# AFNO kernel: inverse DFT on 64 x 64 quarters of the array in plain 32-bit form, and the remainder block spread into its rows by on-chip transfers

## The chip, the cores and the metric

One Trainium2 chip, one core of it. The metric is the device time of one execution of the whole program in microseconds (us). A run with the profiler on leaves a trace, from which all lines marked as profile are taken; times in it count from the first instruction. PE is TensorE with its matmuls, PEld its weight loads, DVE is VectorE, ACT is ScalarE, POOL is GpSimd, SP is SyncE, which here does nothing but issue DMAs in order.

## What is computed

A block of a spectral network over 4096 rows of 640 columns, followed by a SwiGLU feed-forward part. The part that matters here is the spectral one:

```python
def _A_ref(x, w1, b1, w2, b2):
    Xf = jnp.fft.rfft2(x, axes=(1, 2))            # (1, 1, 4096, 640): a real DFT over the 4096 rows
    z = Xf.reshape(B, H, Wf, NB, BS)              # NB = 4 blocks of BS = 160 columns
    hr = relu(zr @ w1[0] - zi @ w1[1] + b1[0])    # one complex layer for each block
    hi = relu(zi @ w1[0] + zr @ w1[1] + b1[1])
    or_ = hr @ w2[0] - hi @ w2[1] + b2[0]         # a second one
    oi_ = hi @ w2[0] + hr @ w2[1] + b2[1]
    # soft shrink of both by 0.01
    return irfft2(or_ + 1j * oi_, s=(H, W), axes=(1, 2))

x = x + ga * _A_ref(layernorm(x) * (1 + ca) + sa)
x = x + gb * ((silu(h @ w_gate) * (h @ w_up)) @ w_down)      # h = layernorm(x) * (1 + cb) + sb
```

The six vectors `sa, ca, ga, sb, cb, gb` come from `silu(c) @ w_mod`. Results are wanted in 32-bit precision.

## The kernel before

**Two steps of the DFT.** 4096 = 128 x 32. A first DFT over 128 points (`dft_a`, L432) is done as matmuls on the normalised rows, whose results go to memory (`s1`, by `write_s1`, L354) and come back as tiles `g`, sorted by frequency. From there the work runs in 8 chunks (`ch`) of 512 frequencies; `tb` holds the constants of a second DFT over 32 points.

**A chunk.** `stage_b` (L594) does the second DFT for the five column tiles of 128: tiles 0 to 3 hold the first 128 columns of the blocks, tile 4 the remainders, the last 32 columns of all four blocks (32 partitions for each). `evac_b` (L603) brings a tile 0 to 3 out of PSUM as `z`, in two parts: a high part rounded to the short form `fp32r` by ACT (L607) and the difference by DVE (L608). The product of two such sums is made of three `fp32r` matmuls instead of one plain 32-bit matmul. `evac_rh` and `evac_rl` (L622, L633) do the same for tile 4, but block by block, for real and imaginary part apart: each instruction takes 32 partitions of PSUM and writes them to the partitions where the first layer wants them. So a tile `rz` for a block holds on 128 partitions: 32 high real, 32 high imaginary, 32 low real, 32 low imaginary. A chunk takes eight instructions on ACT (L630) and eight on DVE (L640) for it.

**The layers.** `stage_l1` (L646) makes three products `pl` for a block: two with eight matmuls (six with `z` and the weights `w1a` and `w1b`, two with `rz` and `w1c`; L661) and one with five (L674), and takes them through the relu to `h` and `r`. `stage_l2` (L695) makes the second layer from them, with frequencies on the partitions, into `tt`, whose two halves are real and imaginary part.

**Back.** `move_x` (L727) copies from `tt` to `xx` by two DMAs on SP, so that real and imaginary part of 64 frequencies stand on 128 partitions. `shrink_parts` and `shrink` (L735, L740) do the soft shrink, `shrink_high` and `shrink_low` (L748, L755) split `xx` into `xh` (ACT, L752) and `xl` (DVE, L757). `stage_i` (L759) does the inverse DFT over 32 points: for each half of the 640 columns three `fp32r` matmuls of 128 x 128 (L768 to L770) with the constants `bm`, an evacuation to `co` (L771), and one DMA from POOL to `s2` (L772). The constants hold zeros outside of two blocks of 64 x 64, as frequencies of odd and of even number do not mix. The last chunk takes another way: `inverse_last` (L815) uses plain 32-bit matmuls on 64 rows of `tt` (L825) with the constants `bx`.

**What sets the order.** All of this stands in a hand-written order (`manual_schedule`), and each engine runs its instructions in that order. The loop at L837 goes over passes `p` = 4 `ch` + `b`: the first layer of pass `p`, second DFT and evacuation for later passes, the second layer of `p - 1`, the shrink of `p - 6` and the inverse DFT of `p - 7`. Ahead of the loop stand the first chunk's `stage_b`, `evac_b` and `evac_r` (L792 to L798). Ahead of these, from L491 to L531, SP gets a long row of DMAs: writes of `s1`, loads of `g` and `tb` of chunk 1, and the constants `idn`, `tx` and `bx`. PSUM tiles come from named banks: `p1`, `p2`, `p3` with two buffers each, and `b0` and `b1`.

After the spectral part (from about 306 us on) the feed-forward part runs. It is the same in both kernels.

Of the kernel before, what the change touches and what calls it, by code (L numbers as in the profile page):

```python
# [6 lines left out]
F32 = mybir.dt.float32  # L7
# [6 lines left out]
P = 128  # L14
# [32 lines left out]
def constants():  # L47
# [8 lines left out]
    fa = np.zeros((N1, 128))  # L56
# [56 lines left out]
    bm = bm.reshape(2, 128, 128)  # L113
    bi = bm[1].reshape(2, 64, 128)

    bx = np.tile(bm[1].reshape(2, 64, 128).transpose(1, 0, 2), (2, 1, 1)).reshape(128, 256)
    bmh, bml = _hl(bm)
    bm = np.stack([bmh, bml], axis=1)
    bm = np.ascontiguousarray(bm.transpose(2, 0, 1, 3)).reshape(128, 2 * 2 * 128)
# [38 lines left out]
def layouts(given):  # L158
    out = {}
    for n in ("A_w1", "A_w2"):  # L160
        w = given[n].transpose(2, 0, 1, 3)
        rows = [w[128:160, ::1 - 2 * (q % 2)] for q in range(4)]
        out[n] = np.ascontiguousarray(np.stack([w[0:128], np.concatenate(rows)]))
# [10 lines left out]
def body(tc, x, w1, b1, w2, b2, wg, wu, wd, c, wm, k_fa, k_tb, k_tx, k_bm, k_bx, k_ga, k_ge, k_id, out, dbg=None):  # L174
# [27 lines left out]
    with ExitStack() as top:  # L202
# [35 lines left out]
        with ExitStack() as af:  # L238
# [4 lines left out]
            bm = wp.tile([P, 2, 2, 128], F32R, name="bm")  # L243
            tx = wp.tile([P, 2], F32, name="tx")
            lp = af.enter_context(tc.tile_pool(name="lp", bufs=1))
            fa = lp.tile([P, 128], F32, name="fa")
# [9 lines left out]
            def prep_weights(raw, wa, wb, wc, split):  # L256
# [11 lines left out]
                for o in range(2):  # L268
                    for oh, ol, n, src in parts(o):
# [6 lines left out]
                                 (wc, h, l, rr[:, o, :, e], 1.0 if o else sgn[:, 0:1])]  # L276
# [63 lines left out]
            with tc.tile_pool(name="sp", bufs=1) as sp:  # L340
# [91 lines left out]
                def dft_a(t):  # L432

                    xnr = xas[t].rearrange("p a (b e) -> p a b e", b=NB)
                    for n, i in enumerate((0, 1, 2, 3, 4) if t < 7 else (4, 0, 1, 2, 3)):
# [3 lines left out]
                        mm(pa, fa, xnr[:, i, :, 0:128] if i < 4 else xnr[:, :, :, 128:160], start=True, stop=True)  # L439
# [15 lines left out]
                for t in range(8):  # L455
# [5 lines left out]
                    if t == 6:  # L461

                        prep1 = prep_weights(raws[1], w1a, w1b, w1c, True)
# [58 lines left out]
            prep2 = prep_weights(raws[2], w2a, w2b, w2c, False)  # L522
# [80 lines left out]
            def evac_b(ch, t):  # L603
                pb = pbs[ch, t]
                z = lp.tile([P, 2, 2, 258], F32R, tag="z", bufs=4, name=f"z{ch}_{t}")
# [10 lines left out]
            def evac_r(ch, b, part=None):  # L616
                if part != 1:
                    evac_rh(ch, b)
                if part != 0:
                    evac_rl(ch, b)  # L620

            def evac_rh(ch, b):  # L622
                pb = pbs[ch, 4]
                if b == 0:
                    rzs[ch] = hp.tile([P, NB, 258], F32R, tag="rz", bufs=2, name=f"rz{ch}")
                    if ch == CE:
                        pool.tensor_copy(rzs[ch][:, :, 257], zero.rearrange("p a b c d -> p (a b c d)")[:, 0:4])
                q = slice(32 * b, 32 * b + 32)
                for i in range(2):
                    act.activation(rzs[ch][32 * i:32 * i + 32, b, 0:256], pb[q, i, :], AF.Identity,  # L630
                                   scale=ca1[q, 4:5])

            def evac_rl(ch, b):  # L633
                pb = pbs[ch, 4]
                r = rzs[ch]
                q = slice(32 * b, 32 * b + 32)
                for i in range(2):
                    rh = slice(32 * i, 32 * i + 32)
                    rl = slice(64 + 32 * i, 96 + 32 * i)
                    dve.scalar_tensor_tensor(r[rl, b, 0:256], pb[q, i, :], ca1[q, 4:5],  # L640
                                             f32(r[rh, b, 0:256]), op0=OP.mult, op1=OP.subtract)
                    if ch == CE:
                        pool.tensor_copy(r[rh, b, 0:257:256], f32(edge[q, 0, 4, i]))
                        pool.tensor_copy(r[rl, b, 0:257:256], f32(edge[q, 1, 4, i]))
# [1894 lines left out]
```

## Time and profile before

| | us |
|---|---|
| median of three runs | 1415.19 |
| the runs | 1413.05, 1418.73, 1415.19 |
| span of the profiled execution, first to last instruction | 1409.5 |
| normalisation and first DFT | 0 to 55.8 |
| first chunk starts | 55.8 to 80 |
| passes of the loop | 80 to 284 |
| last chunk, hand-over | 284 to 306 |
| feed-forward part | 306 to 1409.5 |

The profiled execution's own time is not listed beside its span; the three runs lie 3.6 to 9.2 us over it. The stretches were chosen from the timeline. In a row of the busy time by stretch stand the length, then for each engine the busy time and the number of its instructions, the granted clock of TensorE (1.00 is full), the share of the DMA engines that is busy, and GB/s. In a row of a timeline stand start, length, engine, line, operation, what is written and read, the shape and the number of instructions merged, and in brackets the idle time ahead and what ended it. In a row of one tile or line stand minimum, median and maximum in ns. A matmul lasts longer than the distance to the next one, since matmuls overlap in the array: distances are read from starts.

### The profile page before, as it was taken

The page shows a single profiled execution, that of the slowest core. Times are in us where ns is not written, and L with a number is a line of the kernel's source. Part 1 is how long each engine was busy: PE and PEld are TensorE (multiplying, and loading weights), DVE is VectorE, ACT ScalarE, POOL GpSimd, SP SyncE. Part 2 cuts the span into 40 slices and gives each one's busy share as a digit, 9 for nine tenths or more (in the row PEclk, how much of TensorE's full clock was granted, in tenths as well). Part 3 has the DMA queues.
Part 4 walks back from the last instruction along what each step waited for, and adds up shares of the span by engine and source line. Part 5 has one row for each costly group of instructions (what it writes and reads, how often), then busy time and mean ns, then how long its engine had stood idle before and what let it go on. Part 6 is the DMA issues. An engine that isn't in the chain of part 4 may idle for free. (4 is left out here: it accounts for less than half of the span.)

```text
span 1409.5 us, 23754 instructions
## 1 busy us (share of the span) xinstructions
PE 1382.5 (98%) x8410; PEld 1310.7 (93%) x8410; DVE 1067.8 (76%) x1861; ACT 765.0 (54%) x1542; POOL 604.6 (43%) x683
## 2 busy tenths in 40 slices
PE   6899999999999999999999999999999999999998
PEld 2599999967999889899999999999999999999998
DVE  8889888889888888649787668678678757375644
ACT  6879999755555554436454345546164624262341
POOL 5700200157766594326445534447153624042241
PEclk9999999999999999999999999999999999999999
DMA  9876466675998897898877998696998668956634
GB/s 371 310 244 211 157 196 193 203 232 170 327 353 308 308 335 263 293 368 308 308 225 281 375 330 288 236 326 230 375 330 309 217 218 282 350 194 217 199 115 149
DMA packets 171016, 377.34 MB, mean 268 GB/s; under 512 B 22193, under 2 KB 81649, under 8 KB 168882
## 3 DMA queue, kind: packets, MB, share of 16 engines
q1 hardware_dynamic: 161794, 359.28, 73.6%
q0 software_dynamic: 6800, 13.93, 3.1%
q10 hardware_dynamic: 2304, 2.62, 0.5%
q8 instruction: 66, 1.08, 0.3%
q14 instruction: 52, 0.43, 0.1%
HBM read 269.48 MB, written 96.80 MB: 260 GB/s over the span
## 5 line engine op out<-in xcount | busy, mean ns | idle before, releaser
L1442 DVE TENSOR_TENSOR wb<-r,wb 128x768 fp32r<-128x768 f32 (+3 forms) x170 | 170.4, 1013 | 13.5 <-ACT wb L1435 13.3
L2050 PE MATMUL pw<-h,wt 128*128 128x384 f32 x412 | 139.3, 338 | 0.6 <-ACT s_y L2069 0.6
L2052 PE MATMUL pw<-h,wt 128*128 128x384 f32 x412 | 138.3, 336 | 0.0
L2051 PE MATMUL pw<-h,wt 128*128 128x384 f32 x412 | 138.1, 335 | 0.0
L1435 ACT ACTIVATE wb<-r 128x768 fp32r<-128x768 f32 (+3 forms) x168 | 104.5, 639 | 56.3 <-PE pw L2063 41.7
L2351 PE MATMUL pc<-wq,L 128*128 128x320 f32 x846 | 132.7, 309 | 0.9 <-DMA wq<-wqd 0.9
L2110 POOL TENSOR_TENSOR sg<-s_x,sg 128x384 f32<-128x384 f32 x24 | 30.0, 1250 | 234.5 <-DVE s_x L2076 234.5
L2351 PEld LDWEIGHTS pc<-wq,L 128*128 128x128 f32 x846 | 126.3, 188 | 1.1 <-DVE x L2308 1.1
L2130 DVE TENSOR_TENSOR L<-sg,L 128x384 fp32r<-128x384 f32 x144 | 101.0, 725 | 27.7 <-ACT L L2126 27.2
L2069 ACT ACTIVATE s_x<-pw 128x384 f32<-128x384 f32 x52 | 25.6, 492 | 164.2 <-PE pw L2052 162.3
L2050 PE MATMUL pw<-h,wb 128*128 128x384 f32 x312 | 105.0, 336 | 0.0
L2051 PE MATMUL pw<-h,wb 128*128 128x384 f32 x312 | 104.4, 335 | 0.0
L2052 PE MATMUL pw<-h,wb 128*128 128x384 f32 x312 | 104.4, 335 | 0.0
L2121 POOL TENSOR_TENSOR sg<-sg,sg 128x384 f32<-128x384 f32 x72 | 91.9, 1276 | 23.4 <-DVE L L2130 20.0
L1973 PE MATMUL pg<-ht,wb 128*128 128x512 f32 x260 | 101.8, 392 | 0.0
L2351 PE MATMUL pe<-wq,L 128*128 128x320 f32 x648 | 101.7, 309 | 0.0
L1974 PE MATMUL pg<-ht,wb 128*128 128x512 f32 x260 | 101.3, 390 | 0.0
L1975 PE MATMUL pg<-ht,wb 128*128 128x512 f32 x260 | 101.2, 389 | 0.0
L2267 PE MATMUL pd<-wq,a 128*128 128x320 f32 x632 | 96.8, 310 | 0.0
L2351 PEld LDWEIGHTS pe<-wq,L 128*128 128x128 f32 x648 | 96.6, 188 | 0.0
L2267 PEld LDWEIGHTS pd<-wq,a 128*128 128x128 f32 x632 | 93.5, 188 | 0.5
L772 POOL DMA_DIRECT2D s<-co x28 | 15.7, 559 | 175.9 <-ACT co L771 175.9
(317 smaller groups left out, 3914.1 us busy)
## 6 DMA issues: line engine op xcount, KB each, us to landing
wq<-wqd SPq DMA_DIRECT2D x83, 640.0 KB, 6.1
wt<-td SPq DMA_DIRECT2D x103, 512.0 KB, 5.4
hs<-ho SPq DMA_DIRECT2D x52, 512.0 KB, 5.2
h<-hs SPq DMA_DIRECT2D x32, 768.0 KB, 7.9
td<-wt SPq DMA_DIRECT2D x25, 512.0 KB, 6.3
r<-in_B_w_gate_dram SPq DMA_DIRECT2D x24, 384.0 KB, 4.4
r<-in_B_w_up_dram SPq DMA_DIRECT2D x24, 384.0 KB, 4.3
xx<-tt SPq DMA_DIRECT2D x56, 160.0 KB, 3.3
```

The costliest lines, as they stand in the source:

```text
L1435: def high(ks, e=slice(0, c), copy=lambda o, i: act.activation(o, i, AF.Copy)):
L1442: dve.tensor_tensor(wbs[t, n][:, 1, ks, e], raw[t, n][:, ks, e], f32(wbs[t, n][:, 0, ks, e]), op=OP.subtract)
L1973: mm(b, wh, hh, start=(kk == 0), stop=False)
L1974: mm(b, wh, hl, start=False, stop=False)
L1975: mm(b, wl, hh, start=False, stop=(kk == 4))
L2050: mm(b, w(0, kp), a[:, kp, 0], start=start and kp == 0, stop=False, skip_group_check=not start)
L2051: mm(b, w(0, kp), a[:, kp, 1], start=False, stop=False, skip_group_check=not start)
L2052: mm(b, w(1, kp), a[:, kp, 0], start=False, stop=kp == 1, skip_group_check=not start)
L2121: pool.tensor_tensor(o, x, y, op=op)
L2130: dve.tensor_tensor(o[:, 1], raws[j], f32(o[:, 0]), op=OP.subtract)
L2267: mm(b[:, :320], l, m, start=start and i == 0, stop=stop and i == len(s) - 1)
L2351: mm(o[:, :320], ls[q][:, x, k], w[:, q, y], start=start and q == 0 and n == 0, stop=q == 1 and n == 2, skip_group_check=not start)
```

## The change

1. **Remainder block.** `evac_b` now serves tile 4 too: one instruction on ACT and one on DVE for a chunk, into `z` under a tag of its own (`zr`, one buffer). `move_r` then spreads it by four DMAs on SP, one for each block: 32 partitions with four rows of 256 each go to 128 partitions of `rz`. The rows of `rz` now stand in another order, and the rows of `w1c` with them; their signs come from a column that is added to `fa`.
2. **Inverse DFT.** `bm` holds only the 64 x 64 blocks in plain 32-bit form. `stage_i` takes `xx` directly, by four plain 32-bit matmuls: rows `u` (64 partitions) and columns `e` (320) each pick a quarter of the array. `shrink_high` and `shrink_low` go, and the inverse DFT comes one pass earlier (`p - 6`). The result goes to `s2` by two DMAs on POOL. `move_x` copies with one DMA in place of two. `bm` is loaded by SP, not by POOL.
3. **Order.** Tile 4 is made first in a chunk, also in the first one. `pb` alternates between banks `b0` and `b1`. In the very first block (`ch` = 0, `b` = 0) the products with `z` are issued for all three `pl` ahead of those with `rz`.

```diff
-    fa = np.zeros((N1, 128))
+    fa = np.zeros((N1, 130))
+    fa[:, 128] = (-1.0) ** np.arange(N1)
...
-    bmh, bml = _hl(bm)
...
+    bm = np.stack([bm[:, :, u, :, u].reshape(2, 64, 64) for u in range(2)])
+    bm = bm.reshape(2, 2, 2, 32, 64).transpose(0, 3, 2, 1, 4).reshape(128, 128)
...
-                      bank0(1 if t == 4 else 0, [P, 2, 256], f"pb{ch}_{t}"))
+                      bank0(len(pbs), [P, 2, 256], f"pb{ch}_{t}"))
...
-            def evac_rh(ch, b):
...
-            def evac_rl(ch, b):
...
+            def move_r(ch):
+                rzs[ch] = hp.tile([P, NB, 258], F32R, tag="rz", bufs=2, name=f"rz{ch}")
+                NN = width(ch)
+                for b in range(NB):
+                    nc.sync.dma_start(f32(rzs[ch][:, b, :NN]), f32(zs[ch, 4][32 * b:32 * b + 32, :, :, :NN]))
...
+                if not ch and not b:
+                    for o, n in ((0, 6), (1, 6), (2, 4)):
+                        products(o, 0, n)
...
-                for r in range(2):
-                    nc.sync.dma_start(xx[64 * r:64 * r + 64, :], tts[ch, q][64 * h:64 * h + 64, r, :])
+                nc.sync.dma_start(xx, tts[ch, q][64 * h:64 * h + 64])
...
-            def shrink_high(ch, i):
...
-            def shrink_low(ch, i):
...
             def stage_i(ch, i):
-                xh, xl, _ = xxs[ch, i]
-                for hf in range(2):
...
-                    mm(pi[:, :320], bm[:, kd, 0, :], xh[:, e], start=True, stop=False)
-                    mm(pi[:, :320], bm[:, kd, 0, :], xl[:, e], start=False, stop=False)
-                    mm(pi[:, :320], bm[:, kd, 1, :], xh[:, e], start=False, stop=True)
...
+                for e in range(2):
+                    for u in range(2):
+                        k = slice(64 * u, 64 * u + 64)
+                        mm(pi[u][64 * e:64 * e + 64, :320], bm[k, kd], xx[k, 320 * e:320 * e + 320], start=True, stop=True)
+                for u in range(2):
+                    act.activation(co[:, u], pi[u][:, :320], AF.Copy)
+                for e in range(2):
+                    pool.dma_start(s2[4 * J:4 * J + 4, :, 320 * e:320 * e + 320].rearrange("(u k) n d -> (k n) u d", u=2),
+                                   co[64 * e:64 * e + 64])
...
-            for b, tag in ((0, None), (4, None), (1, "p2")):
+            for b, tag in ((4, None), (0, None), (1, "p2")):
                 stage_b(0, b, tag)
...
+            evac_b(0, 4)
+            move_r(0)
             for b in range(2):
                 evac_b(0, b)
-                evac_r(0, b)
...
-                on(stage_i, p - 7)
+                on(stage_i, p - 6)
...
-                    pool.dma_start(bm.rearrange("p a b c -> p (a b c)"), k_bm)
+                    nc.sync.dma_start(bm.rearrange("p a b -> p (a b)"), k_bm)
```

**SP, where the first chunk starts.** Before, from the last write of `s1` (shown as `s<-xa`) to the first copies of `xx`:

```order
L355 DMA s<-xa_122 64x4x640
L508 DMA idn<-in_k_id_dram 128x128
L509 DMA tx<-in_k_tx_dram 128x2
L531 DMA bx<-in_k_bx_dram 128x256
L308 DMA g_898<-s 128x1x2560
L298 DMA tb_900<-in_k_tb_dram 128x512
L536 DMA wm_0_987<-in_w_mod_dram 128x640
```

Now, from the same write on:

```order
L354 DMA s<-xa_122 64x4x640
L507 DMA idn<-in_k_id_dram 128x128
L508 DMA tx<-in_k_tx_dram 128x2
L530 DMA bx<-in_k_bx_dram 128x256
L619 DMA rz_666<-z_4_663 128x1x256 x4
L862 DMA bm<-in_k_bm_dram 128x128
L619 DMA rz_857<-z_4_854 128x1x256 x4
L307 DMA g_892<-s 128x1x2560
```

The four transfers of the first chunk's `rz` come in behind the load of `bx` and all writes of `s1`, and those of the second chunk ahead of the load of `g`.

**PE, from the second DFT of the first chunk on.** Before (`pb` second DFT, `pl` first layer of block 0):

```order
L600 MATMUL pb_0_646<-tb_408,g_453 128x2x64 x4
L600 MATMUL pb_4_651<-tb_408,g_453 128x2x64 x4
L600 MATMUL pb_1_656<-tb_408,g_453 128x2x64 x4
L661 MATMUL pl_0_0_685<-z_0_663,w1a 128x256 x3
L661 MATMUL pl_0_0_685<-z_0_663,w1b 128x256 x3
L661 MATMUL pl_0_0_685<-rz_666,w1c 128x256 x2
L661 MATMUL pl_0_1_699<-z_0_663,w1a 128x256 x3
```

Now:

```order
L599 MATMUL pb_4_646<-tb_408,g_453 128x2x64 x4
L599 MATMUL pb_0_651<-tb_408,g_453 128x2x64 x4
L599 MATMUL pb_1_656<-tb_408,g_453 128x2x64 x4
L646 MATMUL pl_0_0_684<-z_0_671,w1a 128x256 x3
L646 MATMUL pl_0_0_684<-z_0_671,w1b 128x256 x3
L646 MATMUL pl_0_1_685<-z_0_671,w1a 128x256 x3
L646 MATMUL pl_0_1_685<-z_0_671,w1b 128x256 x3
L646 MATMUL pl_0_2_686<-z_0_671,w1a 128x256 x2
L646 MATMUL pl_0_2_686<-z_0_671,w1b 128x256 x2
L646 MATMUL pl_0_0_684<-rz_666,w1c 128x256 x2
L646 MATMUL pl_0_1_685<-rz_666,w1c 128x256 x2
L646 MATMUL pl_0_2_686<-rz_666,w1c 128x256
```

The 16 products with `z` now stand ahead of the five with `rz`; nothing else of PE stands between them and the second block.

**PE, one call of the inverse DFT in the loop.** Before, between the second layer (`pc`) and the next first layer:

```order
L711 MATMUL pc_2_1_1309<-w2c,r_1_2_1196 128x320 x2
L768 MATMUL pi_0_1320<-xh_0_1210,bm 128x320
L769 MATMUL pi_0_1320<-xl_0_1211,bm 128x320
L770 MATMUL pi_0_1320<-xh_0_1210,bm 128x320
L768 MATMUL pi_1_1325<-xh_0_1210,bm 128x320
L769 MATMUL pi_1_1325<-xl_0_1211,bm 128x320
L770 MATMUL pi_1_1325<-xh_0_1210,bm 128x320
```

Now, at the same place of a pass:

```order
L698 MATMUL pc_1_1_1200<-w2c,r_1_1_1089 128x320 x2
L744 MATMUL pi_0_1211<-xx_0_1044,bm 64x320
L744 MATMUL pi_1_1212<-xx_0_1044,bm 64x320
L744 MATMUL pi_0_1211<-xx_0_1044,bm 64x320
L744 MATMUL pi_1_1212<-xx_0_1044,bm 64x320
L646 MATMUL pl_3_0_1227<-z_3_1019,w1a 128x256 x3
```

Six matmuls of the full array become four on quarters of it, which write two banks in turn.

More of the change, by code (lines that the diff above doesn't have):

```diff
@@ L461, in body @@
                     if t == 6:
[L463 removed]
+                        prep1 = prep_weights(raws[1], w1a, w1b, w1c, True, fa[:, 128:129])
                         for job in prep1[:6]:
@@ L667, in stage_l1 @@
                     hs.append(h)
-                pl = (bank0(1, [P, 512], f"pl{ch}_{b}_2") if 4 * ch + b > LAST else
-                      ps.tile([P, 512], F32, tag="p3", name=f"pl{ch}_{b}_2"))
-                cs = slice(512, 640)
-                seq = [(w1a, z[:, 0, 0, :NN]), (w1a, z[:, 1, 0, :NN]), (w1b, z[:, 0, 1, :NN]),
-                       (w1b, z[:, 1, 1, :NN]), (w1c, r[:, :NN])]
-                for i, (l, m) in enumerate(seq):
-                    mm(pl[:, :NN], l[:, b, cs], m, start=(i == 0), stop=(i == len(seq) - 1))
+                pl = pls[2]
+                products(2, 0 if ch or b else 4)
                 u0 = hp.tile([64, 258], F32, tag="u0", bufs=2, name=f"u0_{ch}_{b}")
```

127 lines of the change are left out of this document (41 added, 86 removed).

## The prediction

> **What bounds the kernel now.** I read the page first, then the busy time by stretch, PE's waits, and last the timelines of PE and SP. Tiles stand without their numbers.
>
> ```profile
> PE 1382.5 (98%) x8410; PEld 1310.7 (93%) x8410; DVE 1067.8 (76%) x1861; ACT 765.0 (54%) x1542; POOL 604.6 (43%) x683
> 55.80:80.00 24.20, 21.29 (x166) 20.50 (x167) 20.40 (x38) 16.58 (x36) 12.30 (x9) 1.00 0.99 372
> 80.00:260.00 180.00, 179.86 (x1408) 178.81 (x1407) 158.10 (x306) 168.39 (x347) 17.51 (x52) 1.00 0.59 189
> 284.00:306.00 22.00, 21.32 (x91) 14.04 (x91) 19.30 (x39) 8.46 (x17) 9.13 (x16) 1.00 0.65 204
> 306.00:1409.50 1103.50, 1092.98 (x6478) 1055.47 (x6475) 801.36 (x1303) 514.00 (x1040) 529.36 (x531) 1.00 0.80 277
> ```
>
> The columns after the length are PE, PEld, DVE, ACT, POOL, clock, DMA share, GB/s. From 80 to 260 us (inverse DFT and both spectral layers) PE is busy 179.86 of 180 us: there only a change of PE's own work counts. From 306 on nothing is edited, and PE is busy 99%: what the first stage gains or loses arrives at the end whole. DMA is full (0.99) from 55.8 to 80, where the first chunk starts. PE's waits there:
>
> ```profile
> PE pc L711 <- DVE r L691: 1.1, 1, 1.1
> PE pb L600 <- DVE z L608: 0.7, 1, 0.7
> PE pc L711 <- DVE w2c L286: 0.5, 1, 0.5
> PE pl L661 <- DVE rz L640: 0.5, 1, 0.5
> ```
>
> **1. The first remainder transfer.** Today ACT and DVE write the rows of `rz` themselves, and PE waits 0.5 us for them. Here are the first evacuation, PE at the first layer, and SP at that time:
>
> ```profile
> 57.01 0.69 ACT L607 ACTIVATE z<-pb,ca 128x512 fp32r<-128x512 f32 x1 [1.76 <-PE pb L600]
> 57.73 0.75 DVE L608 SCALAR_TENSOR_TENSOR z<-pb,ca,z 128x512 fp32r<-128x512 f32 x1 [1.31 <-ACT z L607]
> 58.51 0.60 PE L661 MATMUL pl<-z,w1a 128*128 128x256 f32 x3
> 59.99 0.48 PE L661 MATMUL pl<-rz,w1c 128*128 128x256 f32 x2 [0.52 <-DVE rz L640]
> 60.30 0.51 PE L661 MATMUL pl<-z,w1a 128*128 128x256 f32 x3
> ...
> 61.84 1.05 PE L600 MATMUL pb<-tb,g 128*128 128x128 f32 x8
> 66.30 11.38 SPq L355 DMA_DIRECT2D s<-xa  x10
> 77.72 1.37 SPq L508 DMA_DIRECT2D idn<-in_k_id_dram  x1
> 79.14 1.18 SPq L509 DMA_DIRECT2D tx<-in_k_tx_dram  x1
> 80.42 0.95 SPq L531 DMA_DIRECT2D bx<-in_k_bx_dram  x1
> 81.61 0.57 SPq L308 DMA_DIRECT2D g<-s  x1
> L731 SPq DMA_DIRECT2D xx<-tt x56: 466/591/1482, 92.3 to 268.7; - x56
> DMA to landing us min/median/max: 2.4/3.3/4.8
> ```
>
> The change gives this write to SP. In SP's order (shown with the change) the four transfers of `rz` stand behind the load of `bx`, whose issue ends at 80.42 + 0.95 = 81.37 us; ahead of it SP issues without a pause, ten writes of `s` in 11.38 us. Nothing of the change moves or shortens those. The source is ready long before: the evacuation of the remainder block takes the place of the first one (ACT from 57.01, DVE done at 58.5). So the first transfer is issued at 81.4. No row shows this transfer; the nearest is `xx<-tt`, also from SBUF to SBUF, with 2.4 to 4.8 us to landing. I take its median 3.3: landing at 84.7 (83.8 to 86.2).
>
> PE needs it much sooner. The new order runs 16 products without `rz` first. Thirteen products took 61.84 - 60.30 = 1.54 us, 0.118 each; the low half of `z` is ready about 59.3 (the second ACT step starts when the second block is there, near 57.9, and takes 0.69, DVE 0.75), so they end near 61.2. Then PE's queue is blocked: every later matmul stands behind the five products with `rz`. These end at 84.7 + 5 x 0.118 = 85.3 instead of 61.84: **+23.5 us** (22.6 to 25.0). Nothing covers it, as all of PE's further work hangs on this layer. Behind the transfers on SP stand `bm`, `g` and `tb`, used passes later.
>
> Two smaller terms go with it. DVE makes the weights `w2` during the stall, and the bank of `pb` now alternates, so 1.1 + 0.7 + 0.5 = 2.3 us of waits can go: **-2.3** (0 to -2.3). And PE restarts cold:
>
> ```profile
> L439 PE MATMUL pa<-xa,fa 128*128 128x512 f32 x6 | 5.5, 1088 | 8.0 <-ACT xa L418 8.0
> L439 PE MATMUL pa<-xa,fa x6: 592/592/807, 13.3 to 15.6; 128*128 128x512 f32 x6
> ```
>
> After the idle 8 us at the kernel's start the first six matmuls took 5.3 us (8.0 to 13.3), 0.88 each; the next came 0.46 apart, though the page's granted clock reads full. That loses 6 x 0.42 = 2.5 us. I take **+2.2** (0 to 2.7), as part of the slow stretch falls where PE would wait for ACT anyway. By the Trainium skill (page "TensorE: Matmul & The Clock Gate", section "Part 1: The HAM clock gate") an idle window of about 3.4 us halves PE's clock and a busy one of that length restores it; by that figure the loss would be an estimated 1.7 us, and the trace agrees on the half, not on the length.
>
> **2. The inverse DFT on PE.** 28 calls (one write of `s<-co` each):
>
> ```profile
> L772 POOL DMA_DIRECT2D s<-co x28 | 15.7, 559 | 175.9 <-ACT co L771 175.9
> 203.66 0.31 PE L768 MATMUL pi<-xh,bm 128*128 128x320 f32 x1
> ...
> 204.54 0.52 PE L661 MATMUL pl<-z,w1a 128*128 128x256 f32 x3
> 297.75 1.24 PE L986 MATMUL py<-cfrr,et 128*128 128x320 f32 x4
> 298.82 1.24 PE L983 MATMUL py<-tt,et 128*128 128x320 f32 x4
> 284.81 1.35 PE L825 MATMUL pi<-tt,bx 64*128 64x320 f32 x8 [0.53 <-ACT co L771]
> 286.10 0.41 PE L768 MATMUL pi<-xh,bm 128*128 128x320 f32 x1
> 286.35 0.31 PE L769 MATMUL pi<-xl,bm 128*128 128x320 f32 x1
> 287.51 2.51 PE L825 MATMUL pi<-tt,bx 64*128 64x320 f32 x8
> ```
>
> Now: six matmuls in 204.54 - 203.66 = 0.88 us. After: four plain 32-bit matmuls, each of which PE runs as two (L986: two in the program for each block, four in the trace), at (298.82 - 297.75) / 4 = 0.268 us. One after the other they would take 8 x 0.268 = 2.14 us. But L825 shows two halves of the array at work at once: eight matmuls on 64 rows, half of them on the upper rows, take 1.35 us at 284.81, near 4 x 0.268 + 0.16 = 1.23 (one lasts 1.24 - 3 x 0.268 = 0.43, 0.16 past its slot), and 2.51 where a wait keeps the halves apart. The columns are not split in any row of before. If all four quarters run together the body is 2 x 0.268 = 0.54 us, if only row halves do, 1.07. I take 0.54, plus 0.08 for starts that stand one behind the other.
>
> The switch costs too. At 286.10 PE goes back to the full array: the slot of the last L825 ends at 284.81 + 1.35 - 0.16 = 286.00, so it starts 0.10 late, and its successor comes 0.25 later instead of 0.147: 0.2 us lost. The way in loses 0.12 in the body (1.35 against 1.23); I take 0.15. A call so costs 0.54 + 0.08 + 0.35 = 0.97 us against 0.88: 28 x 0.09 = **+2.5 us**, between 28 x (0.54 - 0.88) = -9.5 (no switch cost) and, with row halves only, 28 x (1.07 + 0.35 - 0.88) = +15.1.
> The Trainium skill (page "TensorEngine Tiling (Array Packing)", section "Key Properties") says "Changing tiling mode (not just tile) drains the TensorE", which speaks against the change; the 0.2 us at 286.10 agrees; without it the term would fall toward the -9.5. The same section lets the tiles load and multiply independently; the trace shows this of the two row halves alone.
>
> **3. Work taken off ACT and DVE.**
>
> ```profile
> L630 ACT ACTIVATE rz<-pb,ca x64: 448/468/472, 57.9 to 260.0; 32x256 fp32r<-32x256 f32 x64
> L640 DVE SCALAR_TENSOR_TENSOR rz<-pb,ca,rz x64: 474/481/496, 58.9 to 261.0; 32x256 fp32r<-32x256 f32 x64
> L752 ACT ACTIVATE xh<-xx x28: 722/723/742, 102.9 to 283.4; 128x640 fp32r<-128x640 f32 x28
> L757 DVE TENSOR_TENSOR xl<-xx,xh x28: 802/814/826, 104.9 to 284.6; 128x640 fp32r<-128x640 f32 x28
> ```
>
> ACT loses 64 x 0.468 + 28 x 0.723 = 50 us, DVE 64 x 0.481 + 28 x 0.814 = 54 us; eight evacuations of the whole block (0.69 and 0.75 us) come in. From 80 to 260 this is worth nothing, as PE is full there. In 284 to 306 DVE is busy 19.3 of 22 us and PE idles 0.7; two of the calls stand in this chain, 0.72 + 0.81 us each: **-1 us** (0 to -2.5). A pass takes (283.4 - 102.9) / 27 = 6.7 us (L752); the later transfers of `rz` are issued three passes ahead of their use, and SP issues as many as before (four of `rz` come, four of `xx` go, for each chunk): 0, and 3.3 us for each of seven chunks if that lead were gone. POOL issues 28 more writes, 15.7 us on an engine with 17.5 of 180 busy, and `co` has three buffers: 0.
>
> **Sum.** +23.5 - 2.3 + 2.2 + 2.5 - 1 = +24.9 us on the profiled span of 1409.5, so 1434.4. The median 1415.19 is 5.7 over that span; with the same offset, **1440 us**.
>
> **Rivals.**
> *Row halves only* (the two column halves of one row half take turns): +15.1 in place of +2.5, 1453 us. For it: no row shows split columns. Against it: nothing here.
> *No switch cost*, PE hiding it behind queued weight loads: -9.5 in place of +2.5, 1428 us. Against it stands 286.10.
> *No overlap at all*: 28 x (2.14 + 0.35 - 0.88) = +45, 1483 us; L825 at 284.81 speaks against it. In this case and the first the change doesn't do what "on quarters" promises.
> *The transfer is hidden*, and the kernel is not slower: decided by the landing of the first `rz`; before 61.2 us there is no stall. Then the waits of 0.5 and 2.3 us go at most: 1415.2 - 2.8 + 2.5 - 1 = 1414 us, and without switch cost 1402. For it: the source is ready at 58.5. Against it: 20 us of SP's rows stand ahead.
>
> **How the numbers follow.** My forecast 0.60; row halves 0.24; no switch cost 0.06; no overlap 0.04; hidden transfer 0.06, of which 0.02 without switch cost. The range takes in the first three: low 1415.2 + 22.6 - 2.3 - 9.5 - 2.5 = 1423, high 1415.2 + 25.0 + 2.7 + 15.1 = 1458. The forecast's own range is 1435 to 1446. 0.5% is 7 us, about what a measurement can tell from no change: faster 0.02, same 0.04, slower 0.94.
>
> **What would show it.** One gap of 22 to 24 us on PE near 61 us that ends with the landing of `rz`, an SP row for `rz` at 81.4, and long matmuls for some microseconds after it; a call of the inverse DFT of about 0.97 us with four matmuls starting close together; the stage from 306 on unchanged but shifted. I am wrong if SP issues `rz` before 61 us, or if a call takes 1.4 us or more.

## The result, and the profile after

The changed kernel takes 1435.22 us (median of 4 runs, 1432.89 to 1435.85) against 1414.47 us for the kernel before on the same chip (4 runs): a ratio of 1.0151, 95% interval 1.0133 to 1.0168. It is slower by 20.75 us, well over the 0.5% that can be told from no change. The profiled execution took 1432.89 us, with a span of 1431.1 us against 1409.5.

Three things can be set beside what was quoted of the kernel before: the engines' shares, the granted clock, and the busy time by stretch. First the profile's busy times and its clock row (one digit for each fortieth of the span; of the kernel before, all 40 are 9), then the stretches, with the columns of before (length, PE, PEld, DVE, ACT, POOL, granted clock, DMA share, GB/s):

```profile
PE 1384.4 (97%) x8466; PEld 1295.4 (91%) x8466; DVE 1022.7 (71%) x1777; ACT 719.0 (50%) x1458; POOL 619.0 (43%) x696
PEclk9879999999999999999999999999999999999999
61.00:82.00 21.00, 0.62 (x3) 0.62 (x4) 0.00 (x0) 0.00 (x0) 7.18 (x7) 0.53 0.96 347
82.00:84.00 2.00, 2.00 (x11) 2.00 (x11) 0.61 (x2) 1.76 (x5) 0.00 (x0) 0.50 0.44 117
86.00:88.00 2.00, 2.00 (x18) 2.00 (x17) 1.94 (x4) 1.76 (x5) 0.00 (x0) 0.93 0.00 0
102.00:280.00 178.00, 178.00 (x1437) 162.38 (x1436) 123.10 (x236) 129.00 (x275) 29.93 (x61) 1.00 0.67 203
326.00:1431.10 1105.10, 1093.82 (x6475) 1056.56 (x6473) 800.17 (x1303) 513.68 (x1040) 528.77 (x529) 1.00 0.80 277
```

DVE and ACT have 45 and 46 us less work, and yet the span is 21.6 us longer. From 61 to 82 us PE does almost nothing, and DVE and ACT nothing; then PE runs at half clock until 86.3, 4.9 us after its restart. From 102 to 280 us it is full, as before. Now PE and SP at the gap, from their timelines (start, length, engine, line, operation; in brackets the idle time ahead and what ended it):

```profile
59.67 0.40 PE L646 MATMUL pl<-z,w1b 128*128 128x256 f32 x2
81.38 1.44 PE L646 MATMUL pl<-rz,w1c 128*128 128x256 f32 x5 [21.30 <-DMA rz<-z]
82.62 1.91 PE L599 MATMUL pb<-tb,g 128*128 128x128 f32 x8
90.94 0.52 PE L646 MATMUL pl<-z,w1a 128*128 128x256 f32 x3
64.03 10.62 SPq L354 DMA_DIRECT2D s<-xa  x10
77.41 1.19 SPq L530 DMA_DIRECT2D bx<-in_k_bx_dram  x1
78.70 2.57 SPq L619 DMA_DIRECT2D rz<-z  x4
```

The products without `rz` end at 60.07. SP works through the ten writes of `s1` and three loads, comes to `rz` at 78.70, and PE starts 2.68 us later. The five products then take 1.24 us instead of 5 x 0.118 = 0.59, and the next group 1.91 us where the same line takes 1.05 at full clock. The row at 90.94 is the start of pass 2.

To see where the 21.6 us come from, the traces are laid side by side by passes. The table shows how much later than in the kernel before the first `pl` product of a pass starts (before: pass 3 at 78.22, pass 7 at 103.04, pass 28 at 253.88, pass 29 at 263.22 us), then the first transpose `pt` of the feed-forward part (305.69), and the span; the other rows are the experiments below.

| kernel | pass 3 | pass 7 | pass 28 | pass 29 | `pt` | span | median, ratio to before [95%] |
|---|---|---|---|---|---|---|---|
| changed | 19.36 | 20.13 | 20.30 | 18.70 | 19.73 | 21.6 | 1435.22, 1.0151 [1.0133, 1.0168] |
| rz by ACT | 20.84 | 21.60 | 21.78 | 20.18 | 21.21 | 23.0 | 1434.12, 1.0166 [1.0143, 1.0188] |
| inverse DFT alone | 4.74 | 5.53 | 5.90 | 4.27 | 5.39 | 8.5 | 1418.28, 1.0050 [1.0034, 1.0066] |
| remainder alone | 22.03 | 22.00 | 21.81 | 21.44 | 20.60 | 26.2 | 1435.71, 1.0172 [1.0152, 1.0192] |
| rz by POOL | 6.44 | 7.45 | 7.62 | 6.03 | 7.01 | 7.1 | 1420.52, 1.0042 [1.0026, 1.0058] |
| rz by POOL, idle tile | 2.19 | 2.96 | 3.13 | 1.53 | 2.36 | 4.1 | 1416.18, 1.0003 [0.9985, 1.0021] |
| inverse DFT, idle tile | 1.27 | 2.07 | 2.42 | 0.79 | 1.89 | 3.4 | 1413.31, 0.9990 [0.9974, 1.0007] |
| in pairs | -1.13 | -0.33 | 0.24 | -0.63 | 0.43 | 3.5 | 1415.09, 1.0008 [0.9994, 1.0022] |
| whole array | -1.25 | -0.40 | 3.37 | 1.94 | 2.13 | 2.9 | 1415.92, 1.0008 [0.9995, 1.0021] |
| pairs outside | 1.20 | 2.00 | -0.29 | -1.15 | -1.37 | -1.2 | 1412.05, 0.9984 [0.9967, 1.0000] |

One of the ten timings of "rz by POOL, idle tile" reads 3527 us; it counts in the median 1416.18 (1415.46 without it) and is left out of the ratio.

For the changed kernel: the start costs 19.4 us; the middle nearly nothing (of 0.9 us, 0.8 come at pass 7, as the first inverse call stands a pass earlier, and go at pass 29); the tail gains, and gives back; the feed-forward part, in which nothing was edited, is 1.8 us longer. Spans of one kernel differ by some microseconds too: 25 runs of the kernel before, on one chip, took 1410.92 to 1420.17 us. So steps are judged by shifts between two places of one trace, and only totals by medians.

### The profile page after: what moved, and what is told of

Read it like the earlier page. It is cut to its first block, busy times and chain, and to the rows that moved or that the text cites. A ratio compares the mean times of both kernels' runs of the same rounds, so it can differ in the third digit from the quotient of the medians.

```text
span 1431.1 us, 23688 instructions
## 1 busy us (share of the span) xinstructions
PE 1384.4 (97%) x8466; PEld 1295.4 (91%) x8466; DVE 1022.7 (71%) x1777; ACT 719.0 (50%) x1458; POOL 619.0 (43%) x696
## 5 line engine op out<-in xcount | busy, mean ns | idle before, releaser
L1400 DVE TENSOR_TENSOR wb<-r,wb 128x768 fp32r<-128x768 f32 (+3 forms) x170 | 174.7, 1038 | 16.1 <-ACT wb L1393 15.8
L748 POOL DMA_DIRECT2D s<-co x56 | 33.5, 602 | 185.2 <-ACT co L746 184.6
```

The costliest lines, as they stand in the source:

```text
L1400: dve.tensor_tensor(wbs[t, n][:, 1, ks, e], raw[t, n][:, ks, e], f32(wbs[t, n][:, 0, ks, e]), op=OP.subtract)
```

## The experiments

**1. The transfer by ACT.** Of the changed kernel, `move_r(0)` is issued by ACT, behind its first three evacuations:

```diff
-            move_r(0)
             for b in range(2):
                 evac_b(0, b)
+            move_r(0)
...
-                    nc.sync.dma_start(
+                    (nc.sync if ch else nc.scalar).dma_start(
```

> The changed kernel, but the four transfers of rz of the first chunk are issued by ACT, behind its evacuations of the first three blocks, instead of by SP behind its ten writes of s1. Theory (the time is lost because SP comes to rz only at 78.7 to 81.3 us): ACT is done with the three blocks near 59.5, issues four transfers in about 2.5 us, each lands some 2.6 us after its issue; PE's gap shrinks from 21.3 to 2 to 5 us, SP has no rz row before chunk 1, and the kernel takes 1416 to 1420 us. Rival A (the time is lost in the inverse DFT on quarters, or the gap is only the place where a later wait shows): 1433 to 1437. Rival B (the DMA engines are full of the s1 writes, so rz lands late on whatever queue): the issue moves to 60 us but the landing stays beyond 70, 1425 to 1435.

No theory hit: 1434.12 us lies in the range of rival A, but the gap on PE is still there (18.5 us, as the first layer itself starts 3 us later), so the run says nothing for or against the inverse DFT. ACT is done at 62.3 us and yet issues only at 77.49. Its timeline, and what the trace has for the line of the transfer (a group with shortest, median and longest time in ns, first and last start):

```profile
61.63 0.69 ACT L606 ACTIVATE z<-pb,ca 128x512 fp32r<-128x512 f32 x1 [0.20 <-PE pb L599]
77.49 5.27 ACTq L619 DMA_DIRECT2D rz<-z  x4
L619 ACTq DMA_DIRECT2D rz<-z x4: 550/551/660, 77.5 to 82.2; - x4
L619 ACTq EVENT_SEMAPHORE  x1: 15822/15822/15822, 61.6 to 61.6; - x1
```

ACT's queue sat 15.8 us on a semaphore. The program's own listing of instructions with their waits says on which (SP's last writes of `s1`, then ACT's transfers):

```
62 L354 DMA s<-xa_118 64x4x640 [waits DMAHW2_49]
63 L354 DMA s<-xa_120 64x4x640 [waits DMAHW3_49]
64 L354 DMA s<-xa_121 64x4x640 [waits DMAHW4_49]
65 L354 DMA s<-xa_122 64x4x640 [waits DMAHW5_49]
...
71 L619 DMA rz_672<-z_4_663 128x1x256 [waits DMAHW3_49,DMAHW2_49,DVE_49]
72 L619 DMA rz_672<-z_4_663 128x1x256 [waits DMAHW3_49]
73 L619 DMA rz_672<-z_4_663 128x1x256 [waits DMAHW4_49]
74 L619 DMA rz_672<-z_4_663 128x1x256 [waits DMAHW5_49]
```

The transfers of SP and ACT take the eight semaphores DMAHW0 to 7 in turn, in the order of the program, and before a semaphore is used again its last transfer must have landed. So the four `rz` wait for the last four writes of `s1`, one by one, (82.2 - 77.5) / 3 = 1.6 us apart. The trace agrees: the second of these writes lands at 79.02, the second `rz` is issued at 79.04. The queue was changed, the place in the turn was not.

**2. The change in halves.** First the inverse DFT alone (ACT and DVE write `rz` as before), then the remainder part alone (the inverse DFT stays three fp32r products on the whole array). The halves are those of the diff above: with the first go `bm`, `move_x`, `stage_i` and the calls at `p - 6`; with the second `move_r`, `zr`, the order of `w1c` and `w2c`, and `products`.

> Only the inverse DFT of the change (quarters in plain 32-bit, xx by one transfer, two writes of s2 by call, a pass earlier); the remainder block is evacuated into its rows by ACT and DVE as before. Theory: no gap at 61 us; a call on PE costs 0.90 instead of 0.88 us (+0.6 us over 28), the tail before the feed-forward part gains about 1.6 us and gives about 1 back to a wait for the reads of s2: 1412 to 1417 us, not told from before. Rival (the switch of the array's form costs the 0.35 us a call that the prediction took, or more): 1417 to 1425.

> Only the remainder part of the change (one evacuation a chunk, transfers of rz on SP, the first 16 products without rz first); the inverse DFT is that of before, three fp32r products on the whole array. Theory: the whole gap of 21 us is there and the kernel takes 1433 to 1438 us, as the changed kernel does. Rival (half or more of the loss comes from the inverse DFT): 1414 to 1426.

The second came out as the theory said: 1435.71 us, the gap is there, and shift and total are near those of the whole change (SP came to `rz` at 80.82 us here, two microseconds later). The first, 1418.28 us, lies over its theory's 1412 to 1417 and in the range of its rival. But the rival, a dearer call of the inverse DFT, does not hold: from pass 8 to pass 28 the shift grows by 0.35 us only, 0.017 a call. The table shows where the time goes: 4.7 us are lost before pass 3. There DVE, and behind it PE, wait for something that has nothing to do with the inverse DFT (the last row is the first `tt` in the kernel before, with no wait ahead of it):

```profile
78.41 0.89 DVE L711 TENSOR_TENSOR tt<-pc,b2t 128x320 f32<-128x320 f32 x2 [8.27 <-DMA s<-xa]
78.96 1.05 PE L709 MATMUL pc<-w2a,h 128*128 128x320 f32 x3 [2.64 <-DVE tt L711]
73.38 0.89 DVE L713 TENSOR_TENSOR tt<-pc,b2t 128x320 f32<-128x320 f32 x2
```

The first write of `tt` waits for a write of `s1`, which reads `xa`. The two share no data, which leaves the memory that they lie in; experiment 3 tests that. The pool `p2` takes over memory that `xa` leaves, and counts from its far end: the change takes two tiles `xh` and two `xl` out of it and gives `co` a third one, six tiles of 2,560 bytes for a partition become three, and all that lies ahead moves up by 7,680 bytes, `tt` on to an `xa` that is still being read. (In the program's allocation the first chunk's `tt` lie on the place of one `xa` in the kernel before and with the idle tile of experiment 3, and across that one and the next in this run and in the changed kernel.) PE's wait is 2.64 us, but pass 3 starts 4.8 us later, measured from pass 2: behind the wait the granted clock reads 0.57 (78.9 to 82.9 us). In the changed kernel no such wait shows: its first `tt` starts at 90.75, as PE is idle till 81.4 anyway.

**3. The transfer by POOL, and the idle tile.** POOL's transfers have completion semaphores of their own (in the trace they are others than those of SP and ACT). The first kernel is that of experiment 1 with the move_r(0) line back in its place and `pool` for `nc.scalar`; the second has the line below too; the third is the inverse DFT alone with that line.

```diff
+                if (ch, i) == (0, 0):
+                    p2.tile([P, 1920], F32, name="gap2")
```

> The changed kernel with the first chunk's four rz transfers issued by POOL, whose transfers have completion semaphores of their own; on ACT they stood idle at the queue's head till 77.5 us, since a transfer issued by ACT takes its turn on the same eight semaphores as SP's and the one ahead, a write of s1, had not landed. Theory 1 (that turn, then, is what held rz): POOL issues near 60 to 62 us, rz lands by 66, PE's gap shrinks to 2 to 5 us. Theory 2, on top of it (seen in the run with the inverse DFT alone: the first tt of DVE waited 8.3 us for a write of s1 that still reads the memory that tt takes over, as p2 is 7,680 bytes smaller and slides on to it): PE waits again near 76 us, pass 3 starts at 83 us (4.7 later than in the kernel before), and the kernel takes 1417 to 1421 us. If only theory 1 holds: pass 3 at 78 to 81 us and 1412 to 1416. Rival (DMA engines full, rz lands late on any queue): landing beyond 75, 1428 to 1436.

> As the run with rz on POOL, and a tile of 7,680 bytes that nothing uses in p2, so that its other tiles lie where they lay in the kernel before. Theory 2 (tt slid on to memory still read by the writes of s1): DVE's first tt no longer waits for s1, the wait of PE near 76 us goes, pass 3 starts 0 to 3.5 us later than in the kernel before, total 1411 to 1416 us. Rival (the wait near 76 has another cause, or rz itself waits on such memory): pass 3 still at 83 us, 1417 to 1421.

> The inverse DFT alone (as before), with the same idle tile of 7,680 bytes. Theory 2: the 8.3 us wait of DVE and the 4.7 us on PE go, pass 3 starts within 1 us of the kernel before, and the kernel takes 1411 to 1415 us, 4 to 6 less than without the tile. Rival: the wait comes from bm now on SP, or from something else of the inverse part: pass 3 at 83 us and 1417 to 1420, as without the tile.

Of the first kernel the rows of POOL and DVE, then PE's longest waits from 55 to 100 us (who waits for whom, us in total, times, longest):

```profile
58.06 2.24 POOL L619 DMA_DIRECT2D rz<-z  x4 [6.74 <-DVE z L607]
80.34 0.89 DVE L700 TENSOR_TENSOR tt<-pc,b2t 128x320 f32<-128x320 f32 x2 [6.96 <-DMA s<-xa]
PE pc L698 <- DVE tt L700: 3.4, 1, 3.4
PE pl L646 <- DMA rz<-z: 2.6, 1, 2.6
```

and of the second, with the idle tile:

```profile
PE pl L646 <- DMA rz<-z: 2.4, 1, 2.4
PE pc L698 <- POOL w2c L527: 1.4, 1, 1.4
```

Both theories hold. POOL issues `rz` at once (58.06), PE starts with it 5.3 us later (63.34), after a gap of 2.6 us: the landing takes longer than the 2.7 us of the changed kernel, but it does not come beyond 75, as the rival had it. But the wait of `tt` comes out from behind it: 3.4 us on PE, and 4.95 from pass 2 to pass 3 (the shift goes from 1.49 to 6.44; the granted clock falls to 0.67 from 80.3 to 84.6), so the kernel is still 0.4% slower. The idle tile takes it away: pass 3 comes 4.3 us earlier, 1416.18 us, no longer told from before. In the inverse DFT alone the same tile brings the ratio from 1.0050 to 0.9990; the rival, `bm` now on SP, falls, as `bm` is there in both. The 1.27 us left at pass 3 hold no wait that the kernel before does not have: PE runs at a granted clock of 0.55 for three microseconds there (columns of the stretches, as above):

```profile
71.00:74.00 3.00, 3.00 (x17) 3.00 (x16) 2.91 (x6) 1.03 (x3) 0.00 (x0) 0.55 1.04 401
```

**4. The price of the quarters.** In the first kernel the four products of each call are made twice; in the second the inverse DFT (with the idle tile) runs on the whole array in plain 32-bit form; `xx` and `s2` move as in the kernel before.

```diff
-                for e in range(2):
+                for e in (0, 1, 0, 1):
```

```diff
-                for e in range(2):
-                    for u in range(2):
-                        k = slice(64 * u, 64 * u + 64)
-                        mm(pi[u][64 * e:64 * e + 64, :320], bm[k, kd], xx[k, 320 * e:320 * e + 320], start=True, stop=True)
+                for u in range(2):
+                    mm(pi[u][:, :320], bm[:, kd], xx[:, 320 * u:320 * u + 320], start=True, stop=True)
```

> The changed kernel with the four quarter products of every call of the inverse DFT done twice, the second time into the same place. Theory (a round of four quarters holds PE for 2 x 0.268 us, since all four run at once, and the other 0.36 us of the 0.90 is the change of the array's form, paid once a call): each call 0.54 us longer, passes 8 to 28 drift by 0.54 us each against the changed kernel (10.7 us over twenty), the kernel 14 to 16 us longer, 1448 to 1452. Rival A (the 0.36 is paid by each round): 0.90 a call, 18 us over twenty passes, 1459 to 1462. Rival B (row halves or columns take turns): 1.07 a call, 1464 to 1467.

> The inverse DFT alone with the idle tile, but its product is made on the whole array in plain 32-bit form, with the block-diagonal 128x128 matrix (two matmuls a call, no change of the array's form, xx and s2 moved as in the kernel before). Theory: 4 x 0.268 = 1.07 us a call and nothing for a change of form, against 0.90 on quarters: passes 8 to 28 drift by +0.17 us each, the kernel takes 4 to 5 us more than the run with the idle tile, 1416 to 1419. Rival (the 0.36 us is not the change of form but the plain 32-bit products' own start or end, so the whole array pays it too): 1.43 us a call, +0.53 a pass, 1426 to 1430.

One call on PE in each of the three kernels, changed, twice, whole array; the row ahead and the second group behind are there to measure between (the first group behind, three products of `z` with `w1a`, is left out of the rows):

```profile
231.23 0.46 PE L698 MATMUL pc<-w2c,r 128*128 128x320 f32 x2
231.62 0.77 PE L744 MATMUL pi<-xx,bm 64*64 64x320 f32 x8
232.78 0.52 PE L646 MATMUL pl<-z,w1b 128*128 128x256 f32 x3
```

```profile
238.48 0.46 PE L698 MATMUL pc<-w2c,r 128*128 128x320 f32 x2
238.87 1.31 PE L744 MATMUL pi<-xx,bm 64*64 64x320 f32 x16
240.56 0.52 PE L646 MATMUL pl<-z,w1b 128*128 128x256 f32 x3
```

```profile
213.20 0.46 PE L708 MATMUL pc<-w2c,r 128*128 128x320 f32 x2
213.49 1.24 PE L755 MATMUL pi<-xx,bm 128*128 128x320 f32 x4
214.93 0.53 PE L658 MATMUL pl<-z,w1b 128*128 128x256 f32 x3
```

From the row ahead to the group behind: 1.55, 2.08 and 1.73 us. A second round of quarters costs 0.53 us, two slots of 0.268: all four quarters work at once. Over many calls it is the same: from pass 8 (130.07 us) to pass 27 (278.01) the doubled kernel needs 10.24 us more than the changed one (129.82, 267.52), 0.54 for each of 19 calls. The total is 1446.46 us in its one run, just under the range expected. The whole array loses 0.162 us a call against the quarters (pass 8 at 109.45 and pass 28 at 257.25, against 111.75 and 256.31 with quarters and the idle tile: 3.24 us in 20 calls; 1.73 - 1.55 = 0.18 in the rows above), near the expected 0.17: its four slots are 1.07 us, so the quarters cost 0.91, 0.54 of it work and 0.37 the change of form. The doubled kernel, which pays no more than 0.54 for its second round, shows that this is paid once at each visit. The total with the whole array is 1415.92 us, just under the expected range, and 2.6 more than with quarters on another chip; those intervals overlap, so the trace decides here.

**5. The cold restart.** Of the changed kernel, PE runs matmuls on ones during the gap; they add work that feeds nothing.

```diff
                     for o, n in ((0, 6), (1, 6), (2, 4)):
                         products(o, 0, n)
+                    idle(85)
```

> The changed kernel with 85 idle 128x128 matmuls (0.224 us each, 19 us) on PE in the gap, between the products without rz and those with it; they add work that feeds nothing. Theory (the PE restarts cold and loses about 2.3 us): the matmuls after the gap come 0.12 us apart from the first on instead of 0.21, and the kernel takes 1432.5 to 1433.5 us, 2 less than the changed one. Rival (the slow stretch is covered by waits for ACT, DVE and the weights that PE would have had anyway): the pitch is 0.12 but the later passes start no earlier, 1435.

> The changed kernel with 97 idle matmuls in the gap; the 85 of the run before (0.235 us each, 20 us) ended 4.2 us ahead of the landing of rz, so that PE was slow again 0.9 us after its restart and the run decided little. Theory (cold restart): with the matmuls reaching to within 2 us of the landing no slow stretch follows, and from the first product with rz to the first product of pass 2 it takes about 7.3 us, against 9.56 in the changed kernel and 8.91 with 85. Rival (the stretch would have been filled by waits for the weights and the evacuations): 8.5 us or more although the matmuls are 0.12 us apart.

The 85 matmuls missed: they ended 4.18 us ahead of the landing, which came at 83.67 in that run, and PE slowed down again soon after its restart. With 97 they reached to within 1.36 us:

```profile
60.61 21.82 PE L333 MATMUL pz<-ones 128*128 128x128 f32 x194
83.79 0.86 PE L646 MATMUL pl<-rz,w1c 128*128 128x256 f32 x5 [1.36 <-DMA rz<-z]
84.48 1.05 PE L599 MATMUL pb<-tb,g 128*128 128x128 f32 x8
91.44 0.52 PE L646 MATMUL pl<-z,w1a 128*128 128x256 f32 x3
```

From the first product with `rz` to the first of pass 2 it now takes 91.44 - 83.79 = 7.65 us, against 9.56 (81.38 to 90.94) in the changed kernel: the cold clock costs 1.9 us, net of the waits that it covers. The total does not show it (1436.17 us in one run; 1437.05 with 85): SP came to `rz` some two microseconds later in these runs (80.48 and 80.94), and the feed-forward part of both traces took 4.7 us longer than before, not 1.8.

**6. Two calls at a visit.** Since the change of form is paid at each visit, two calls at one should save one of the two. Built on the inverse DFT with the idle tile; `inverse_mm` holds the quarter products of `stage_i`, `inverse_out` its evacuations and writes, and the calls left over after pass 28 stay single:

```diff
-                on(stage_i, p - 6)
+                if p % 2 == 0 and p > 5:
+                    stage_i(*[divmod(k, 4) for k in (p - 7, p - 6) if k >= 0])
...
+                for n, (ch, i) in enumerate(calls):
+                    inverse_mm(ch, i, pis, "p1" if n < len(calls) - 1 else "p3")
+                for ch, i in calls:
+                    inverse_out(ch, i, pis[ch, i])
```

> The inverse DFT alone with the idle tile, and up to pass 28 two calls of the inverse DFT stand together in every second pass (eight quarter products one behind the other in four banks, then the evacuations). Theory (0.54 us of quarters a call, and 0.36 us for the change of the array's form once per visit): a pair costs 1.44 instead of 1.80 us, so eleven pairs gain 4.0 us of PE: passes 8 to 28 drift by -0.36 us for each pair against the run with the idle tile, and the kernel takes 1408 to 1411 us, 3 to 5 less than both kernels. Rival A (the first layer's banks p1 come free too late, as ACT has four copies of 0.45 us to make ahead of it): each pair waits 0.4 us or more, no gain, 1412 to 1416. Rival B (the 0.36 is paid for each call, as between two different tiles of xx): no drift.

Up to pass 16 it works, with less gain than the 0.36 us expected for a pair: passes 8, 10, 12, 14 and 16 start at 108.58, 122.42, 136.54, 151.52 and 164.54 us, with single calls at 111.75, 125.87, 140.24, 155.47 and 168.74: -3.17, -3.45, -3.70, -3.95, -4.20, a gain of 0.26 for each pair. Then passes 18 and 20 lose about 4 us, and the total misses its 1408 to 1411: 1415.09 us. PE's waits from 100 to 260 us:

```profile
PE pi L761 <- DVE tt L721: 1.1, 2, 0.6
PE pl L659 <- DVE tt L721: 0.9, 1, 0.9
```

From the start ahead of such a wait to the start behind it 1.30, 1.26 and 1.34 us pass, 3.9 in all. L721 reads the third product group that only the middle chunk has, from a bank of `p1`, the one that the pair's first call borrows. So the last kernel keeps single calls there (the middle chunk is `CE` = 4, its second layer runs in passes 17 to 20), and lets ACT issue one of the last call's two writes:

```diff
+                if 4 * CE < p < 4 * CE + 5:
+                    one_i(p - 6)
+                elif p % 2 == 0 and p > 5:
...
-                    pool.dma_start(
+                    (nc.scalar if 4 * ch + i == LAST - 1 and e == 0 else pool).dma_start(
```

> As the run with calls in pairs, but single calls in passes 17 to 20, where the second layer of the middle chunk has a third product group in a bank of p1, and one of the two writes of s2 of the last call by ACT instead of both by POOL. In the run with pairs the five pairs up to pass 16 gained 0.25 us each over the run with the idle tile, and passes 18 and 20 lost some 4 us, with waits of PE for DVE's read of that bank. Theory: no such wait now, nine pairs gain 2 to 3 us, the first layer's pass 28 starts 2.5 to 4 us earlier than in the run with the idle tile (counted from the same pass 5), the kernel takes 1410 to 1412.5 us, 0.15 to 0.3 per cent less than before: the interval may or may not leave out 1. Rival (the loss at passes 18 and 20 came from the pairs themselves, xx held too long or ACT's four copies): waits at passes 22 to 28 of the same size, 1413 to 1416. The write by ACT: PE's wait for the reads of s2 near 295 us (about 1 us) falls to under 0.5, or stays if it was not POOL's issue that was late.

No wait for L721 is left, and pass 28 starts 2.65 us earlier than with single calls (2.72, less 0.07 that were there at pass 5), as expected. But 0.8 of it are a call that is still owed there. At pass 29, where both have made the same calls, 1.9 us are left: nine pairs gain 0.21 each, a little under the 2 to 3 us expected. And with one write issued by ACT, PE's wait for the reads of `s2` is gone. It takes 1412.05 us, ratio 0.9984, interval 0.9967 to 1.0000: the lowest median of all, two microseconds under the kernel before, at the edge of what these runs can tell.

## Why the prediction was right, step by step

**The transfer of `rz` (+23.5).** Right in place and kind: one gap that ends with the landing of `rz`, an SP row for `rz` behind `bx`. The size was too large: counted as in the prediction, the next `pb` group starts at 82.62 instead of 61.84, 20.8 us later, of which 0.65 is slow clock; so the term is 20.1, under its range of 22.6 to 25.0. The start as a whole costs 18.5 to 22.0 us at pass 3 in the kernels that have the gap, not 23.4. There are two reasons. SP came to `rz` at 78.70 instead of 81.4: the prediction took the row ahead as fixed, but SP started its ten writes 2.3 us earlier than in the profile of before (64.03 against 66.30) and took 10.62 us for them, not 11.38; in the other runs with this row it came at 78.19 to 80.94. And PE could start 2.7 us after the issue, not 3.3, near the lower end of the `xx<-tt` that it was taken from. Experiments 2 and 3 show that this wait, and the order behind it, is the cause: the remainder part alone brings it all, and `rz` by POOL takes 12.9 us of it away (19.36 to 6.44 at pass 3), the idle tile 4.3 more.

**Waits recovered (-2.3) and cold restart (+2.2).** The shift falls from 21.53 us at pass 1 to 19.35 at pass 2, by 2.2 us. But part of the slow clock, which lasts to 86.3, lies in this stretch too. With PE kept busy (experiment 5) the shift falls from 22.6 to 19.8: the waits that go are worth 2.8 us, and the restart costs 1.9 by the one run with 97 matmuls. Both terms are right in kind and near in size.

**The inverse DFT (+2.5).** Mechanism right, size off: 0.54 for the body and 0.35 to 0.37 for the change of form were as predicted, but the 0.08 on top, for starts one behind the other, is not there. From pass 8 to pass 28 the shift moves from 20.16 to 20.30 us, 0.007 a call, so the term is under 0.5 us instead of 2.5. The rivals with row halves only, without overlap and without switch cost fall with experiment 4.

**Work off ACT and DVE (0, and -1 in the tail).** From pass 7 to pass 28 the shift stays within 0.4 us, though the two engines lost 45 us each: worth nothing there. At pass 29 it falls by 1.6, of which 0.8 is the call moved earlier; the other 0.8, by subtraction, is the term. But a step was missing: the last call's write of `s2` is now two, issued one behind the other by POOL, and the reads of `s2` wait for both.

```profile
307.60 1.19 POOL L748 DMA_DIRECT2D s<-co  x2 [4.31 <-ACT co L746]
312.49 0.33 SPq L810 DMA_DIRECT2D cfrm<-s  x1
PE py L946 <- DMA cfrm<-s: 1.0, 1, 1.0
```

PE waits 1.0 us there and did not before; the last kernel, with ACT issuing one of the two, does not either. "POOL issues 28 more writes: 0" held for the middle and not for the last one.

**The feed-forward part (0).** It came out 1.8 us longer. This is hardly the change's: in the kernels of the table, none of which edits this part, it is 0.1 to 5.6 us longer than before (span less `pt`). The last section shows what is behind the 1.8.

**The rival "hidden transfer" (1414 us)** was priced too low. The run with `rz` by POOL comes near its condition, and took 1420.52 us: behind the gap stood the wait of `tt` for memory, which nobody who reads only the trace of before can see. With the idle tile it is 1416.18.

So the sum: 19.4 at the start (23.4 predicted), 0.9 in the middle (2.5), -1.6 + 1.0 in the tail (-1), 1.8 in the feed-forward part (0): 21.6 us of span, but for rounding. The measured 1435.22 us lies at the very edge of the forecast's own range, 1435 to 1446, and it does so with the help of those 1.8 us, for which the prediction had no term. The mechanism was right; that the number falls inside the narrow range is in part luck.

## What to carry to other kernels

A move of work from an engine to a transfer is priced by where the transfer stands: behind what on the issuing queue, behind which uses of the completion semaphores, and whether its place at the start of the loop is the same as in the middle. A tile added to or taken out of a pool moves the others; where a pool takes over memory that transfers still read, look at the first write of each tile for a new wait, and if one is there, give the size back: 7,680 idle bytes took 4.3 us away here. A change of the array's form is paid for each visit, so gather the work of several calls into one visit, in banks that nothing else claims at that time.

## What the runs showed of the hardware

A wait of two microseconds can cost PE nearly as much again. In the changed kernel PE waits 1.97 us at once for `chl` in the feed-forward part, where before it waited 0.89 us for `ht` and, 7.7 us later, 0.79 for `chl`. From 345.7 us, 0.8 after the wait, PE runs at half clock, for 3.4 us. PE's row, the stretch behind it (columns as above), and the same stretch of before:

```profile
344.91 0.41 PE L1646 MATMUL py<-chl,gt 128*128 128x320 f32 x1 [1.97 <-DVE chl L1636]
345.00:349.20 4.20, 4.20 (x14) 3.45 (x15) 3.96 (x7) 1.90 (x4) 0.00 (x0) 0.59 1.06 394
325.30:328.00 2.70, 2.70 (x14) 2.36 (x15) 2.70 (x6) 1.60 (x3) 0.00 (x0) 1.00 0.86 239
```

The same 14 matmuls take 4.20 us and 2.70. The loss, about 1.5 us, is most of the feed-forward part's 1.8. Whether a wait has this price varies between runs: ahead of the slow stretch at 71 us in the inverse DFT with the idle tile stand waits of 1.08 and 0.54 us; waits of 1.07 and 0.53 us for the same things cost no clock in the kernel before. Of the 25 runs of the kernel before on one chip, those with a mean granted clock of 1.000 took 1410.92 to 1414.06 us, those with 0.996 1416.11 to 1420.17. The Trainium skill (page "TensorE: Matmul & The Clock Gate", section "Part 1: The HAM clock gate") has the clock halved after an idle window of about 3.4 us that runs freely, and restored after a busy one. Half clock for 3.4 us agrees with this trace, and a window that runs freely would make the price vary as it does; a wait of 1.97 us that is enough does not fit a window of 3.4 us that must be idle throughout.

Four quarters of the array do work at once. PE runs a plain 32-bit matmul as two; over 320 columns each of the two takes a slot of 0.268 us on the whole array, and on four quarters at once it takes the same (experiment 4: 0.53 to 0.54 us for a round).
